# A planned kernel: two-bank copies, short spins, paired score matmuls, a new load plan, and a last store in halves

## The chip, the cores and the metric

The kernel runs on one core of one Trainium2 chip. Times are device microseconds (us) of that core. A kernel is quoted by the median of its fast runs with their range. A ratio is the mean time of one kernel's fast runs over that of the kernel before in the same rounds on the same chip, so it is not quite the ratio of the quoted medians. Executions over 1.5% slower than the fastest of the same kernel are left out of the means. A profile is one execution, and its "span" is some 2 us shorter than the time. TensorE is PE in the profile (PEld: its weight loads), VectorE DVE, ScalarE ACT, GpSimd POOL, SyncE SP.

## The reference

An RWKV5 attention over 24 chunks (4 batch rows, 6 chunks of 128 steps) is followed by a mixture of four experts, each applied to every row.

```python
cur   = einsum('bhd,bhe->bhde', u * k_t, v_t)
y_t   = einsum('bhd,bhde->bhe', r_t, state + cur)
state = w * state + einsum('bhd,bhe->bhde', k_t, v_t)
...
p = domain_probs / (domain_probs.sum(-1) + 1e-9)      # 3072 rows, 4 experts
out += p[:, e] * (relu(x @ w1[e]) @ w2[e])            # 384 -> 1024 -> 384
```

The inputs r, k, v are 4 x 8 x 768 x 48 in fp32. The weights are 12.6 MB in fp32, cast to bf16 on the chip.

## The kernel before

The program is a set of jobs. While it builds, it plays them through on a model of the five engines and the DMA queue, with an assumed duration for each. The order in which jobs begin in that play is the order in which each engine gets its instructions. On the chip the order is fixed, and an engine whose next instruction has no data waits. I call the play "the plan".

```python
def load_in(n, ci):  load_job((n, ci), (0.97, 64), run, ...)              # 192 KB: 0.97 us of queue assumed
def load_w(m, e, i):                                                      # a weight piece of 2 or 3 blocks
    us = 0.615 * (bb - a) + (0.4 if i == 0 else 0.0) + (0.5 if (m, e, i) == (1, 0, 0) else 0.0)
ORDER = "K0 V0 K1 V1 R0 K2 R1 R2 w1e0.0 w1e0.1 K3 ...".split()            # order of the loads on SyncE
...
def cast(m, e, i, rank):      # staged fp32 -> bf16 weights: a job of ACT, DVE or POOL
    job(("cast", m, e, i), on, run, [("wst", m, e, i)], rank, (), (("wst", m, e, i),))
...
# scores of one chunk: both halves of its transposed R and K from one PSUM bank, copied out by ACT and DVE
for q in range(NP):
    for j in range(2):
        nc.tensor.matmul(tl["At", ci, j][:, q, :], ..., start=True, stop=True)   # 8 matmuls, 64 rows
...
spin(NSPIN)                   # 11 filler matmuls of 512 columns at the start, for the clock
for t, _, e, j in started:    # the plan, played out
    if e == "T":
        slow = 2.0 if t < WARM else 1.0
        n = int((t - pe_end - 0.2) / (0.22 * slow) * 0.6)
        if t < 30 and n > 0:
            spin(min(n, 8))   # fillers of 512 columns where the plan has TensorE idle
```

## Time and profile before

| | before |
|---|---|
| time, median of 3 runs | 301.76 us (301.3 to 302.39) |
| span of the profiled run | 299.2 us |
| first scores / first hT / end of last matmul | 10.28 / 18.61 / 295.80 us |
| first expert's second matmul ("out") | 25.84 us |
| end of last matmul to end of span | 3.39 us |

hT is the first matmul of an expert (x times w1), out the second. Y is the attention output of a chunk, X its transpose, from which the experts start. This is the chain of work that ended last, by line, in shares of the span:

```profile
PE out_ps L577 42%; PE hT_ps L550 35%; PE hT_ps L544 5%; PE At_ps L417 3%; PE Y_ps L448 2%; PE RKT_ps L381 1%; DMA Rt<-in_r_dram 1%; DVE w_sb L74 1%; PE Y_ps L441 1%; PE St_ps L489 1%; PE spin_ps L170 1%; SPq L188 1%; DVE RK L324 1%; PE xT_ps L474 1%; DVE S L502 0%
```

The table of windows: length, then busy us and count of PE, PEld, DVE, ACT, POOL; then clock, DMA share, GB/s.

```profile
26.00:60.00 34.00, 33.73 (x347) 22.01 (x348) 29.61 (x53) 22.29 (x36) 16.61 (x21) 1.00 1.01 274
60.00:90.00 30.00, 29.84 (x333) 20.37 (x333) 22.92 (x42) 22.13 (x37) 23.44 (x31) 1.00 0.90 215
```

And the waits between 26 and 92 us (total, times, longest): this is the largest on a load.

```profile
POOL dv L363 <- DMA Vt<-in_v_dram: 10.7, 2, 8.3
```

TensorE is busy for all but 0.4 us of these 64 us, while the DMA queues are about full. There are waits of POOL on inputs.

### The profile page before, as it was taken

To read this page: it belongs to the slowest core of one execution; us is meant where nothing else is said; L and a number is where in the kernel's file an instruction comes from. 1 tells how busy PE (TensorE), PEld (TensorE's weight loads), DVE (VectorE), ACT (ScalarE), POOL (GpSimd) and SP (SyncE) were. 2 spreads that over 40 slices of the span, in tenths; PEclk is the share of its full clock that TensorE was granted. 3 is DMA by queue.
4 is the path that set the end of the run, shared out by engine and by line. 5 is a ranking of instruction groups with operands and counts; after the bars stand their busy time and mean duration, and the time that the engine had idled before them with its cause. 6 is when DMAs were issued, how large, how long until landed. Compare 5 with 4: busy or idle time off the path is not lost.

```text
span 299.2 us, 5668 instructions
## 1 busy us (share of the span) xinstructions
PE 288.9 (97%) x2216; PEld 167.0 (56%) x2244; DVE 157.3 (53%) x299; ACT 152.3 (51%) x253; POOL 100.5 (34%) x136
## 2 busy tenths in 40 slices
PE   7699999999999999999999999999999999999995
PEld 2377557688545655555555455555555555555553
DVE  3776879987866736445556435555414422101223
ACT  5376865585683043554533464434465344565430
POOL 1866164677976623253253244231000000000000
PEclk9789999999999999999999999999999999999999
DMA  7998999998987083662462771421232000200002
GB/s 151 275 306 240 325 246 269 229 241 209 244 174 146 16 186 101 167 127 45 84 127 54 180 129 37 96 49 37 96 71 50 0 13 28 79 0 2 0 0 105
DMA packets 108110, 36.92 MB, mean 123 GB/s; under 512 B 96282, under 2 KB 108060, under 8 KB 108084
## 3 DMA queue, kind: packets, MB, share of 16 engines
q1 hardware_dynamic: 108068, 36.56, 51.1%
q8 instruction: 17, 0.28, 0.4%
q14 instruction: 9, 0.07, 0.1%
q10 hardware_dynamic: 16, 0.00, 0.0%
HBM read 26.79 MB, written 4.72 MB: 105 GB/s over the span
## 4 chain that ended last, share of the span: by engine, by line
PE 91%; DVE 4%; DMA 1%; issue 1%; SPq 1%; ACT 0%; DVEq 0%; ACTq 0%
PE out_ps L577 42%; PE hT_ps L550 35%; PE hT_ps L544 5%; PE At_ps L417 3%; PE Y_ps L448 2%; PE RKT_ps L381 1%; DMA Rt<-in_r_dram 1%; DVE w_sb L74 1%; PE Y_ps L441 1%; PE St_ps L489 1%; PE spin_ps L170 1%; SPq L188 1%; DVE RK L324 1%; PE xT_ps L474 1%; DVE S L502 0%
## 5 line engine op out<-in xcount | busy, mean ns | idle before, releaser
L561 ACT ACTIVATE hTs<-hT_ps 128x512 bf16<-128x512 f32 x168 | 99.6, 598 | 104.5 <-PE hT_ps L550 100.0
L577 PE MATMUL out_ps<-w_sb,hTs 128*128 128x384 bf16 x768 | 140.1, 326 | 0.2 <-DVE w_sb L74 0.2
L550 PE MATMUL hT_ps<-xTe,w_sb 128*128 128x512 bf16 x476 | 122.5, 379 | 1.5
L577 PEld LDWEIGHTS <-hTs 128*128 128x128 bf16 x768 | 72.7, 98 | 52.2 <-DVE w_sb L74 0.7
L587 DVE SCALAR_TENSOR_TENSOR oacc<-out_ps,p_nat,oacc 128x384 f32<-128x384 f32 x72 | 44.3, 617 | 91.3 <-PE out_ps L577 90.2
L550 PEld LDWEIGHTS <-w_sb 128*128 128x128 bf16 x504 | 47.0, 98 | 47.0 <-DVE w_sb L74 0.3
L426 DVE TENSOR_TENSOR AtM<-At_ps,mask 128x512 bf16<-128x512 f32 x48 | 31.0, 684 | 19.8 <-PE At_ps L417 19.8
L363 POOL TENSOR_TENSOR dv<-Vt,dcoef 128x384 f32<-128x384 f32 x24 | 21.5, 896 | 50.8 <-DVE Ysb L457 32.3
L337 POOL TENSOR_TENSOR ruk<-Rt,Kt 128x384 f32<-128x384 f32 x24 | 24.6, 1025 | 40.2 <-DMA Kt<-in_k_dram 33.2
L345 POOL TENSOR_TENSOR ruk<-ruk,U_sd 128x384 f32<-128x384 f32 x23 | 24.0, 1046 | 1.2
L585 ACT ACTIVATE oacc<-out_ps,p_nat 128x384 f32<-128x384 f32 x24 | 14.0, 582 | 14.1 <-PE out_ps L577 13.8
L457 DVE TENSOR_TENSOR Ysb<-Y_ps,dv 128x384 bf16<-128x384 f32 x24 | 13.3, 555 | 13.2 <-PE Y_ps L448 11.3
L559 ACT ACTIVATE hTs<-hT_ps 128x512 bf16<-128x512 f32 x24 | 14.1, 600 | 9.3 <-PE hT_ps L544 8.7
L509 POOL TENSOR_TENSOR S<-Tn,wC 64x192 bf16<-64x192 f32 x32 | 16.1, 503 | 7.1 <-DVE Tn L504 5.9
L544 PE MATMUL hT_ps<-xTe,w_sb 128*128 128x128 bf16 x288 | 18.2, 219 | 0.0
L544 PEld LDWEIGHTS <-w_sb 128*128 128x128 bf16 x288 | 16.6, 98 | 0.9 <-DVE p_nat L294 0.2
L324 DVE TENSOR_TENSOR RK<-Rt,W_sd 128x384 bf16<-128x384 f32 x20 | 14.2, 714 | 0.0
L504 DVE TENSOR_TENSOR Tn<-S,St_ps 64x192 f32<-64x192 bf16 x32 | 11.2, 350 | 5.6 <-PE St_ps L489 4.8
L358 DVE TENSOR_REDUCE dcoef<-ruk 128x8 f32<-128x384 f32 x24 | 13.0, 542 | 0.1
L76 POOL CAST Vb<-Vt 128x384 bf16<-128x384 f32 x20 | 10.7, 541 | 6.5 <-PE St_ps L489 4.9
L72 ACT CAST w_sb<-wst 128x1152 bf16<-128x1152 f32 (+1 forms) x13 | 12.8, 1003 | 0.0
L324 DVE TENSOR_TENSOR RK<-Kt,W_sd 128x384 bf16<-128x384 f32 x20 | 12.7, 635 | 0.0
(63 smaller groups left out, 136.8 us busy)
## 6 DMA issues: line engine op xcount, KB each, us to landing
wst<-in_moe_w_dram SPq DMA_DIRECT2D x16, 576.0 KB, 6.5
Kt<-in_k_dram SPq DMA_DIRECT2D x24, 192.0 KB, 3.9
Vt<-in_v_dram SPq DMA_DIRECT2D x24, 192.0 KB, 5.6
Rt<-in_r_dram SPq DMA_DIRECT2D x24, 192.0 KB, 4.1
out_dram<-oacc SPq DMA_DIRECT2D x24, 192.0 KB, 1.9
wst<-in_moe_w_dram SPq DMA_DIRECT2D x8, 384.0 KB, 5.4
RKT<-RK SPq DMA_TRANSPOSE x14, 3.2
xTe<-Ysb SPq DMA_TRANSPOSE x14, 2.5
```

Source lines behind the costliest of these rows:

```text
L324: eng.tensor_mul(RK[:, i, :, 0:D], tl[("Kt", "Rt")[1 - i], ci], tl["W", i] if ci < SUB and i not in on_pool else W_sd[i])
L337: nc.gpsimd.tensor_mul(tl["ruk", ci], tl["Rt", ci], tl["Kt", ci])
L345: nc.gpsimd.tensor_mul(tl["ruk", ci], tl["ruk", ci], U_sd)
L363: nc.gpsimd.tensor_mul(tl["dv", ci], tl["Vt", ci], tl["dcoef", ci].to_broadcast((128, H, D)))
L426: nc.vector.tensor_mul(tl["AtM", ci][:, j], tl["At", ci, j], mask[:, None, :].to_broadcast((128, NP, C)))
L509: nc.gpsimd.tensor_mul(S_new[pr, :, cl], tl["Tn", ci][pr], wC[pr, :, None].to_broadcast((P2, NP, D)))
L544: nc.tensor.matmul(ps[:, i, :], w1_sb[:, e, db, (fb + i) * 128:(fb + i + 1) * 128], xTe[:, db, s0, :], start=(i == 0 and db == 0), stop=(i ...
L550: nc.tensor.matmul(ps[:, 0:n, :].rearrange("p a b -> p (a b)"), w1_sb[:, e, db, fb * 128:(fb + 1) * 128], xTe[:, db, s0:s0 + n, :].rearran ...
L559: nc.scalar.activation(hTs[:, fb:fb + 4, s0, :], ps, AF.Relu)
L561: nc.scalar.activation(hTs[:, fb, s0:s0 + n, :], ps[:, 0:n, :], AF.Relu)
L577: nc.tensor.matmul(ps, tl["hTs", e, sc][:, fb, s, :], w2_sb[:, e, fb, :], start=(fb == 0), stop=(fb == NFB - 1))
L587: nc.vector.scalar_tensor_tensor(tl["oacc", ci], in0=tl["o", e, ci], scalar=pe, in1=tl["oacc", ci], op0=ALU.mult, op1=ALU.add)
```

## The change

The intent: let the two copies of a transpose result overlap (two PSUM banks in place of one), fill TensorE's idle time at the start with shorter spins so that the clock stays up, pay the entry and exit of a score stretch once for two chunks, shorten the last evacuation and store, and take a new load order. With the load order come shorter assumed load durations, 5% less for inputs and 14% less for weights.

```diff
-        load_job((n, ci), (0.97, 64), run, (("inp", ci),))
+        load_job((n, ci), (0.92, 64), run, (("inp", ci),))
...
-        us = 0.615 * (bb - a) + (0.4 if i == 0 else 0.0) + (0.5 if (m, e, i) == (1, 0, 0) else 0.0)
+        us = 0.53 * (bb - a) + (0.3 if i == 0 else 0.0) + (0.5 if (m, e, i) == (1, 0, 0) else 0.0)
...
-    ORDER = ("K0 V0 K1 V1 R0 K2 R1 R2 w1e0.0 w1e0.1 K3 w1e0.2 V2 R3 w2e0.0 w2e0.1 p V3 w2e0.2 R4 K4 "
+    ORDER = ("R1 R0 K1 V1 K0 V0 K2 w1e0.0 R2 w1e0.1 w1e0.2 R3 V2 p K3 w2e0.0 V3 w2e0.1 R4 K4 w2e0.2 "
...                                                            (the rest of the order differs too)
+            two = ci < SUB
...
+                    if two:
+                        tl["T", ci, i] = psum.tile([128, NP, C], BF16, tag=("tr", "At")[i], bufs=i + 1,
+                                                   name="RKT_ps")
...
+        paired = ci >= DMAT
...
+            for x in (ci - 1, ci) if paired else (ci,):
+                for j in range(2):
+                    tag = ("tr", "mm")[j] if paired and x == ci else "At"
...
+            if (e, ci) == (E - 1, TOTC - 1):
+                last_chunk(e, ci, rk + 2, groups)     # second matmul, evacuation, store: two halves
+                continue
...
-                slow = 2.0 if t < WARM else 1.0
-                n = int((t - pe_end - 0.2) / (0.22 * slow) * 0.6)
-                if t < 30 and n > 0:
-                    spin(min(n, 8))
+                n = int((t - pe_end - 0.05) / 0.056)
+                if t < 24 and n > 0:
+                    spin(n, 1)                        # one block of 128 columns, not four
```

Not shown: RKT gets four buffers for three, Tn two for three, and the first chunk of a pair moves to the slot of the second.

## The prediction

> **What bounds the kernel now.** I read the page first: busy shares, the row of the granted clock, and the chain that ended last.
>
> ```profile
> PE 288.9 (97%) x2216; PEld 167.0 (56%) x2244; DVE 157.3 (53%) x299; ACT 152.3 (51%) x253; POOL 100.5 (34%) x136
> ...
> PEclk9789999999999999999999999999999999999999
> ...
> PE 91%; DVE 4%; DMA 1%; issue 1%; SPq 1%; ACT 0%; DVEq 0%; ACTq 0%
> ```
>
> TensorE (PE) is 97% busy and 91% of the chain that sets the end; no other engine passes 53%. The clock row has one dip, in its second and third slice. So the kernel is matmul bound, and only what shortens TensorE's sequence, or starts it earlier, can count. The table of windows tells where TensorE is not doing real work:
>
> ```profile
> 5.00:10.00 5.00, 2.70 (x14) 1.08 (x13) 1.78 (x4) 2.44 (x6) 1.41 (x2) 1.00 1.07 199
> 10.00:15.00 5.00, 3.93 (x40) 2.52 (x41) 4.04 (x9) 2.09 (x6) 4.83 (x6) 0.55 1.01 316
> 15.00:20.00 5.00, 5.00 (x55) 3.42 (x54) 3.58 (x8) 3.52 (x6) 3.15 (x4) 0.76 1.12 301
> ...
> 100.00:150.00 50.00, 49.68 (x343) 27.21 (x347) 26.49 (x50) 22.61 (x38) 17.89 (x25) 1.00 0.49 107
> ```
>
> From 100 us on TensorE lacks 0.3 us in 50. But in 5:10 it is busy for 2.70 us of 5, in 10:15 for 3.93 at a granted clock of 0.55, in 15:20 all the time but at 0.76. Finer windows (a quarter of a microsecond each) put the dip from 10.5 to 17.35 us, at 0.50 throughout. I added up what the sequence needs at the full-clock spacings of the trace (out 768 x 0.1625 us, 512-wide hT 504 x 0.216, 128-wide hT 288 x 0.056, At 24 visits x 0.42, Y 24 x 0.20 + 20 x 0.17, state 20 x 0.17, transposes 110 x 0.056, set-up 2.3): 280.0 us. The last matmul issues at 295.6, so 15.6 us are lost, 6.8 of them before the first transpose at 8.28 us, some 7 between there and the first expert matmul at 18.61, and only about 2 in all the rest. The start shows why, in the timeline of all engines:
>
> ```profile
> 9.17 0.59 ACT L72 COPY RKT<-RKT_ps 128x512 bf16<-128x512 bf16 x1 [1.80 <-PE RKT_ps L381]
> ...
> 9.79 0.42 DVE L74 COPY RKT<-RKT_ps 128x512 bf16<-128x512 bf16 x1 [0.50 <-ACT RKT L72]
> ...
> 14.87 1.03 PE L381 MATMUL RKT_ps<-ident,RK 128*128 128x128 bf16 x8
> ...
> 15.70 2.28 PE L170 MATMUL spin_ps<-spin_in 128*128 128x512 bf16 x6
> 15.94 0.42 DVE L74 COPY RKT<-RKT_ps 128x512 bf16<-128x512 bf16 x1 [1.35 <-PE RKT_ps L381]
> ...
> 16.40 0.59 ACT L72 COPY RKT<-RKT_ps 128x512 bf16<-128x512 bf16 x1 [0.75 <-DVE RKT L74]
> ...
> 16.74 1.28 DVE L426 TENSOR_TENSOR AtM<-At_ps,mask 128x512 bf16<-128x512 f32 x2
> 16.88 1.89 ACT L72 CAST w_sb<-wst 128x1152 bf16<-128x1152 f32 x2
> ...
> 18.61 0.84 PE L544 MATMUL hT_ps<-xTe,w_sb 128*128 128x128 bf16 x12
> ```
>
> The two copies of one transpose result never overlap: at 9.79 VectorE (DVE) had waited for ScalarE (ACT), at 16.40 ScalarE for VectorE, 0.5 and 0.75 us. The eight transposes at 14.87 take 1.03 us at half clock. Six filler matmuls ("spins") take 2.28 us. The cast of the second weight piece, which the first hT needs, starts only at 16.88, behind the delayed copy. Further on the cost of a score visit can be read from TensorE's timeline:
>
> ```profile
> 155.50 0.81 PE L550 MATMUL hT_ps<-xTe,w_sb 128*128 128x512 bf16 x3
> 156.25 0.40 PE L417 MATMUL At_ps<-RKT 64*128 64x128 bf16 x8
> 156.57 0.82 PE L550 MATMUL hT_ps<-xTe,w_sb 128*128 128x512 bf16 x3
> ```
>
> Three hT issue from 155.50 and are done issuing after 3 x 0.216 at 156.15; the scores start at 156.25 and the next hT at 156.57. The visit costs 0.42 us. Its eight matmuls start within 0.40 - 0.216 = 0.18 us, so eight are worth 0.21, and 0.21 is the price of going in and out. Last, the end:
>
> ```profile
> 295.83 0.62 DVE L587 SCALAR_TENSOR_TENSOR oacc<-out_ps,p_nat,oacc 128x384 f32<-128x384 f32 x1 [0.68 <-PE out_ps L577]
> ```
>
> After this evacuation of 0.62 us the last store is issued at 296.48; its packets run from 297.31 to 297.99, the landing is seen at 298.33, and the span ends at 299.2.
>
> **What the Trainium skill says.** TensorE: Matmul & The Clock Gate, Part 1 (the HAM clock gate): the clock is either full or half, set by how busy TensorE was in a free-running window, about 3.4 us long. The trace agrees on the two levels (0.50 and 1.00, nothing between); its one low stretch lasts 6.83 us, twice that window. TensorEngine Tiling (Array Packing), Key Properties: changing the tiling mode drains TensorE. The trace agrees: 64-row scores between 128-row matmuls pay the 0.21 us. PSUM — Partial Sum Buffer, section PSUM bank collisions raise a hardware error: two engines must not touch one bank at once, even to read, so the program orders them by bank. The trace agrees: the 0.5 and 0.75 us waits between the copies. DMA: Bandwidth & Descriptors, Anatomy of one DMA: a fixed part of about 2 us, mostly the write receipt, that halving a transfer leaves alone. Here 1.85 us pass from issue to landing, 0.68 of them packets.
>
> **The change, part by part.**
>
> *Scores in pairs.* The instruction order of the changed kernel has ten score stretches of 8 and seven of 16, no other matmul within a stretch. A pair should cost 0.21 + 2 x 0.21 = 0.63 in place of 0.84, so 7 x 0.21 = **1.5 us** off a saturated TensorE. The cost is one of the four "mm" banks until the fourth mask is done, 4 x 0.68 + 0.2 = 3 us later. In the order, three hT (1.95 us) and an out (1.3) follow the pair, then Y and more; the waits listed for them are on ScalarE's relus and on an evacuation that precedes the masks in VectorE's order. Y of the second chunk comes about 5.9 us after the pair. I expect no stall, at most 0.1 us a pair.
>
> *The last chunk in halves.* TensorE does the same columns (16 x 0.0825 for 8 x 0.1625). The last evacuation has half the elements: about 0.42 for 0.62 if some 0.2 us of it are fixed, an estimate. The last store's packets take half: -0.3. **0.45 us**.
>
> *The start.* Loads begin R1 R0 K1 V1 K0 V0; K0, which completes chunk 0, is the fifth load as R0 was before, so lands at the same 7.57. R of chunk 0 is scaled and transposed before it. From there I walk the new orders of each engine with the durations of the trace, the clock taken as full; a load is taken to land when the trace had moved as many bytes as stand ahead of its end in the new order, plus the 0.8 us that R of chunk 0 took from its last byte (6.78) to its use (7.57). K scaled to 8.22, its transposes done at 8.7; VectorE does ruk (to 9.3), then its copy (9.7); ScalarE has V0's cast first (V0 lands sixth, about 8.7), then its copy, to 9.87. Scores at 9.93 (10.28 before). Masks behind two reductions 10.8 to 12.1; Y at 12.2 (12.45). Copies of chunk 1 in parallel by 13.75, X of chunk 0 at 13.9 behind 17 spins, scores of chunk 1 at 14.2. Their masks now precede the next copy on VectorE: 14.8 to 16.1 (before 16.74 to 18.02). ScalarE casts piece one at 11.75 and piece two, landing about 14.2, by 15.4. So the first hT runs at about **15.9**, 2.7 us earlier. Then masks, POOL's scale of K3 (its load lands at 18) and two copies of chunk 3 on ScalarE pace it: the sixth hT group, after which all first hT of three chunks, four transposes and four score visits are done, ends near 23.5; the same work is done at 25.84 in the kernel before (its four small p transposes included). Gain **2.3 us**. After that the second-matrix pieces, then expert 1's, are needed 2.3 us earlier, while the DMA queues are nearly full (share 1.0 from 10 to 24, one hole at 24 to 26). I let 0.5 us go there: **1.8 us**.
>
> Sum with a full clock: 301.8 - 1.5 - 0.45 - 1.8 = 298.0.
>
> **The rivals.**
>
> *The clock still drops.* 100 spins of 128 columns take 5.6 us at full clock, but 30 of them stand between the first scores and Y, 17 before X. At half clock these are 3.2 and 1.8 us: Y moves from 12.2 to 13.5, X to 16.6, the first hT to about 19, so the start loses some 0.5 us instead of gaining. For it: spins cannot fill the wait for K0 (7.4 to 8.3), and before, a window that was 56% busy was not enough. Against it: the same stretch becomes about 77% busy, by the walk above. Result 300.3. I give it 0.3.
>
> *The start's gain is hidden by weights.* If expert 0's second matrix and expert 1's pieces arrive no earlier, TensorE waits in 24 to 36 us for what it gained, and only 1.5 + 0.45 and perhaps 0.5 remain: 299.3. For it: the DMA share. Against it: the hole at 24 to 26, and only 0.8 us of TensorE loss in 25 to 45 before.
>
> *The shared bank stalls TensorE.* If each pair costs the 0.2 us that it saves, the pairs are worth nothing and the time is 299.5. The order's waits speak against it, and four score banks masked in one go hold VectorE for 2.7 us only where it was 53% busy.
>
> **Range and chances.** The full-clock case (0.7) centres on 298.0, the half-clock case on 300.3, either with the weights as a spread of about 1 us. I predict **298.3 us**, 8 times in 10 from **296.5** to **300.6**. Two per cent faster is 295.7; for that the start would have to yield over 4 us of the 9 lost there after 8.28, which the casts forbid: 0.06. Slower by 2% would need a stall at every pair and a lost start: 0.02. Within 2%: 0.92.
>
> **What would show it.** Right: seven score stretches where the gap from the last hT issued to the next is 0.63; no TensorE idle time over 0.1 us after them; a granted clock of 1.00 from about 4 us on; the first hT near 15.9; copies of one chunk that overlap; a last evacuation near 0.42 and a last store with 0.34 us of packets. Wrong: a clock row with a 6.8 us dip, spins on the chain of waits before Y or X, waits of out_ps or hT_ps on casts between 23 and 36 us, or waits of hT_ps on masks.

## The result, and the profile after

The changed kernel takes **302.12 us** (301.87 to 302.36, 4 runs), the kernel before 301.88 us in the same rounds; the ratio is 1.0008 (95% interval 0.9988 to 1.0029). It is the same within 2%, as I gave 0.92 to, but the time lies outside the range of 296.5 to 300.6. The profiled span is 300.1 us against 299.2.

The page of the changed kernel, busy shares, clock row and the two lines of the chain:

```profile
PE 294.4 (98%) x2342; PEld 174.1 (58%) x2342; DVE 154.3 (51%) x299; ACT 153.5 (51%) x253; POOL 102.5 (34%) x137
...
PEclk9999999999999999999999999999999999999999
...
PE 92%; DVE 4%; DMA 2%; SPq 1%; issue 0%; ACT 0%; DVEq 0%
PE out_ps L624 39%; PE hT_ps L594 36%; PE spin_ps L170 4%; PE hT_ps L588 4%; PE At_ps L428 2%; DMA wst<-in_moe_w_dram 2%; PE RKT_ps L386 2%; DVE RK L324 1%; PE Y_ps L466 1%; PE St_ps L507 1%; PE Y_ps L459 1%; SPq L200 1%; PE u_ps L257 1%; PE w_ps L253 1%; PE out_ps L557 0%
```

TensorE looks even busier, and the clock row has no dip. Two things stand out in the chain: spins, 4% where they were 1%, and weight loads (wst), 2%, which the chain before did not have. The clock row misleads: its first record in this run comes at 13.86 us. How long TensorE's work took says what the clock was before, in the timeline:

```profile
9.44 1.35 PE L170 MATMUL spin_ps<-spin_in 128*128 128x128 bf16 x11
...
13.83 1.85 PE L170 MATMUL spin_ps<-spin_in 128*128 128x128 bf16 x30
...
16.14 0.42 DVE L74 COPY RKT<-RKT_ps 128x512 bf16<-128x512 bf16 x1 [0.46 <-PE RKT_ps L386]
...
16.36 0.59 ACT L72 COPY RKT<-RKT_ps 128x512 bf16<-128x512 bf16 x1 [2.53 <-PE RKT_ps L386]
...
19.03 0.83 PE L588 MATMUL hT_ps<-xTe,w_sb 128*128 128x128 bf16 x12
```

Eleven spins take 1.35 us at 9.44, 0.12 each; thirty take 1.85 us at 13.83, 0.06 each. So the clock was half until 13.86, where the kernel before had it released at 3.70 and then lost it from 10.5 to 17.35. The copies at 16.14 and 16.36 do overlap, as intended. The first hT comes at 19.03, not 18.61.

The windows of the changed kernel, start, weight time and steady state:

```profile
5.00:10.00 5.00, 5.00 (x16) 1.82 (x15) 1.03 (x2) 1.99 (x5) 1.99 (x2) 1.00 1.03 209
10.00:15.00 5.00, 5.00 (x61) 4.61 (x59) 2.97 (x6) 3.00 (x7) 3.03 (x4) 1.00 1.12 334
15.00:20.00 5.00, 5.00 (x99) 4.63 (x95) 4.40 (x10) 3.12 (x6) 3.47 (x4) 1.00 1.06 251
26.00:60.00 34.00, 33.70 (x384) 23.85 (x382) 28.29 (x55) 24.54 (x37) 17.83 (x25) 1.00 1.04 278
60.00:90.00 30.00, 28.74 (x300) 18.95 (x299) 22.95 (x39) 18.13 (x28) 22.36 (x26) 1.00 0.90 216
100.00:150.00 50.00, 50.00 (x356) 27.58 (x354) 24.51 (x49) 23.79 (x40) 20.05 (x28) 1.00 0.53 111
```

From 60 to 90 us TensorE is busy 28.74 us where it was 29.84. The waits between 26 and 92 us have two lines at their top that the kernel before has not:

```profile
DVE w_sb L74 <- DMA wst<-in_moe_w_dram: 6.9, 4, 2.6
ACT w_sb L72 <- DMA wst<-in_moe_w_dram: 6.0, 4, 2.8
```

A cast that waits doesn't stop TensorE by itself, but what stands behind it in the same engine's order does. The timelines of DVE, ACT and TensorE at 81 to 87 us:

```profile
81.33 1.14 DVE L74 CAST w_sb<-wst 128x768 bf16<-128x768 f32 x1 [2.62 <-DMA wst<-in_moe_w_dram]
...
84.08 0.83 ACT L72 CAST w_sb<-wst 128x768 bf16<-128x768 f32 x1 [2.85 <-DMA wst<-in_moe_w_dram]
...
84.94 0.68 DVE L437 TENSOR_TENSOR AtM<-At_ps,mask 128x512 bf16<-128x512 f32 x1
...
86.07 0.68 DVE L437 TENSOR_TENSOR AtM<-At_ps,mask 128x512 bf16<-128x512 f32 x1
...
86.80 0.27 PE L466 MATMUL Y_ps<-Vb,AtM 128*128 128x48 bf16 x4 [0.85 <-DVE AtM L437]
```

DVE stood still for 2.62 us until the weights of that cast were there; the masks of scores that were done at 80.9 came after it and after two more jobs, and Y waited 0.85 us for the second mask.

The score stretches of two chunks, in TensorE's timeline:

```profile
158.86 1.46 PE L624 MATMUL out_ps<-w_sb,hTs 128*128 128x384 bf16 x8
160.26 0.62 PE L428 MATMUL At_ps<-RKT 64*128 64x128 bf16 x16
160.81 2.12 PE L594 MATMUL hT_ps<-xTe,w_sb 128*128 128x512 bf16 x9
```

Eight out issue until 158.86 + 8 x 0.1625 = 160.16, and hT starts at 160.81: 0.65 us for two chunks, for which the kernel before paid 2 x 0.42. And the last evacuation is 0.42 us where it was 0.62:

```profile
297.07 0.42 DVE L562 SCALAR_TENSOR_TENSOR oacc<-out_ps,p_nat,oacc 128x192 f32<-128x192 f32 x1 [0.24 <-PE out_ps L557]
```

To see where the time went I kept the ledger of the prediction running: each matmul counts as its full-clock spacing, in the order in which it issues (records missing from a trace filled in from the program's order), and "lost" is the time passed minus that. Spins count nothing. Unlike in the prediction's 280.0 us, eight score matmuls count as 0.21 us here, so that the way in and out of a score stretch is in "lost".

| lost by TensorE, us | to 26 us | 26 to 90 us | 90 to 290 us | last matmul to span's end |
|---|---|---|---|---|
| before | 15.84 | 1.96 | 2.96 | 3.39 |
| changed | 16.62 | 3.80 | 1.53 | 3.07 |
| difference | +0.78 | +1.84 | -1.43 | -0.32 |

The sum, +0.87, is the difference of the two spans (+0.91) but for the few us after 290 that are left out. The late gains came almost as predicted; the start gained nothing in this run, and 1.84 us went between 26 and 90 us.

### The profile page after: what moved, and what is told of

Its sections match the earlier page's. It is cut to its first block, busy times and chain, and to the rows that moved or that the text cites. A ratio compares the mean times of both kernels' runs of the same rounds, so it can differ in the third digit from the quotient of the medians.

```text
span 300.1 us, 5903 instructions
## 1 busy us (share of the span) xinstructions
PE 294.4 (98%) x2342; PEld 174.1 (58%) x2342; DVE 154.3 (51%) x299; ACT 153.5 (51%) x253; POOL 102.5 (34%) x137
## 2 busy tenths in 40 slices
DMA packets 108255, 36.94 MB, mean 123 GB/s; under 512 B 96298, under 2 KB 108204, under 8 KB 108228
## 4 chain that ended last, share of the span: by engine, by line
PE 92%; DVE 4%; DMA 2%; SPq 1%; issue 0%; ACT 0%; DVEq 0%
PE out_ps L624 39%; PE hT_ps L594 36%; PE spin_ps L170 4%; PE hT_ps L588 4%; PE At_ps L428 2%; DMA wst<-in_moe_w_dram 2%; PE RKT_ps L386 2%; DVE RK L324 1%; PE Y_ps L466 1%; PE St_ps L507 1%; PE Y_ps L459 1%; SPq L200 1%; PE u_ps L257 1%; PE w_ps L253 1%; PE out_ps L557 0%
## 5 line engine op out<-in xcount | busy, mean ns | idle before, releaser
L437 DVE TENSOR_TENSOR AtM<-At_ps,mask 128x512 bf16<-128x512 f32 x48 | 30.3, 682 | 25.0 <-PE At_ps L428 25.0
L363 POOL TENSOR_TENSOR dv<-Vt,dcoef 128x384 f32<-128x384 f32 x24 | 20.2, 843 | 43.8 <-DVE Ysb L475 30.7
L632 ACT ACTIVATE oacc<-out_ps,p_nat 128x384 f32<-128x384 f32 x24 | 13.9, 582 | 15.6 <-PE out_ps L624 15.6
L527 POOL TENSOR_TENSOR S<-Tn,wC 64x192 bf16<-64x192 f32 x32 | 18.1, 564 | 7.1 <-DVE Tn L522 5.9
L72 ACT CAST w_sb<-wst 128x1152 bf16<-128x1152 f32 (+1 forms) x13 | 13.7, 1051 | 6.1 <-DMA wst<-in_moe_w_dram 6.0
L170 PE MATMUL spin_ps<-spin_in 128*128 128x128 bf16 (+1 forms) x111 | 13.9, 285 | 1.1 <-DVE spin_in L90 1.1
L324 DVE TENSOR_TENSOR RK<-Kt,W_sd 128x384 bf16<-128x384 f32 x20 | 13.9, 695 | 0.1
L324 DVE TENSOR_TENSOR RK<-Rt,W_sd 128x384 bf16<-128x384 f32 x20 | 13.7, 685 | 0.2
```

The lines of the kernel that those rows point to most:

```text
L170: nc.tensor.matmul(ps[:, 0:m, :], spin_in, spin_in[:, None, :].to_broadcast((128, m, 128)), start=True, stop=True)
L324: eng.tensor_mul(RK[:, i, :, 0:D], tl[("Kt", "Rt")[1 - i], ci], tl["W", i] if ci < SUB and i not in on_pool else W_sd[i])
L363: nc.gpsimd.tensor_mul(tl["dv", ci], tl["Vt", ci], tl["dcoef", ci].to_broadcast((128, H, D)))
L437: nc.vector.tensor_mul(tl["AtM", ci][:, j], tl["At", ci, j], mask[:, None, :].to_broadcast((128, NP, C)))
L527: nc.gpsimd.tensor_mul(S_new[pr, :, cl], tl["Tn", ci][pr], wC[pr, :, None].to_broadcast((P2, NP, D)))
```

## The experiments

**Theory A:** the start's gain is lost because the clock was released at 13.86 us instead of some 4 us; release it in time, and the predicted time comes. **Theory B:** what the start gains is given back between 26 and 90 us, because weights do not arrive earlier and the fixed orders of DVE and ACT make TensorE wait behind casts. Later experiments split B: is it the new load order, or the shorter assumed durations? The three sets of runs were on three chips; before took 301.39, 301.69 and 301.35 us there (7 runs each).

### 1. A longer opening: after_spin15

```diff
-    WARM, NSPIN = 5.4, 11
+    WARM, NSPIN = 5.4, 15
```

> The changed kernel with 15 opening spins in place of 11, nothing else. In the profile of the changed kernel the clock was released at 13.86 us, in that of before at 3.70, and the 11 spins ended at 5.7 at half clock. Fifteen spins at 0.427 us keep TensorE on 128-row matmuls beyond 7.04, the end of the next window. Theory A, the late release is what ate the start: clock 1.00 from about 7.0, first scores near 10.9 in place of 13.3, first hT 16.3 to 16.6 in place of 19.0, and the time 1.5 to 2.5 us below the changed kernel's 302.1, so 299.6 to 300.6. Rival B, the waits on weights at 70 to 90 us set the end whatever the start does: first hT as early, but the loss at 70 to 90 grows from 2.3 us and the time stays within 0.5 of 302.1. Rival C, more spins only delay: first hT later, time up by 1 us.

Measured: 302.63 us (301.89 to 303.57), ratio 1.0042 (1.0005 to 1.008). In its profile the clock is released at 4.17 us and stays. Scores start at 9.93, Y at 11.94, X at 13.55, the first hT at 15.47. The walk of the prediction had 9.93, 12.2, 13.9 and 15.9, so it was right for a full clock. The ledger to 26 us stands 1.67 us better than before. And yet the last matmul ends at 297.06, as in the changed kernel (297.03): 6.30 us are lost between 26 and 90. The waits of casts are now the largest:

```profile
ACT w_sb L72 <- DMA wst<-in_moe_w_dram: 12.8, 8, 4.1
DVE w_sb L74 <- DMA wst<-in_moe_w_dram: 10.5, 6, 2.9
```

TensorE's window from 60 to 90 us is no better than the 28.74 us of the changed kernel:

```profile
60.00:90.00 30.00, 28.25 (x293) 18.77 (x296) 22.90 (x39) 18.00 (x28) 22.43 (x27) 1.00 0.96 228
```

What TensorE gained, the casts waited longer. Theory A falls as the cause of the miss; B stands, with the size still to be shown.

### 2. The old spin rule: after_oldspins

The changed kernel with the spin rule of the kernel before (the last lines of the diff undone).

> The changed kernel with the old spins (512 columns, few) in place of the short ones, the rest as changed. The new loads give back what the start wins or loses (theory B), so the time stays within 0.7 of 302.1, though the clock shows a half-rate dip again (mean clock under 0.99) and the first hT moves to anywhere from 16 to 19.5. Rival: short spins carry the start, and without them the time rises by over 1 us.

Measured: 302.24 us (300.4 to 303.05), ratio 1.0012 (0.9969 to 1.0055). The clock dips from 8.22 to 11.64, but the first hT is at 15.18 and the last matmul ends at 297.11; casts wait 21.6 us for weights. So short spins are not what makes the early start (the rest of the change is enough), and the gain is given back just the same. No run undoes the two-bank copies alone.

### 3. No pairs: after_nopairs

```diff
-        paired = ci >= DMAT
+        paired = False
...
-            e_g, sc_g, one = SLOTS[ci - LEAD - (ci % 2 if ci >= DMAT else 0)]
+            e_g, sc_g, one = SLOTS[ci - LEAD]
```

> The changed kernel with the pairing of the scores undone (every score stretch of 8 matmuls, two banks), nothing else. If a pair saves the price of one way in and out, 7 x 0.21, the time rises by 1.5 us to 303.6, and TensorE's loss at 100 to 250 us rises from 1.3 to 2.7. If the shared bank cost as much as it saved, the time stays at 302.1.

Measured: 303.59 us (301.97 to 304.24), ratio 1.0065 (1.0022 to 1.0107), 1.5 us over the changed kernel's 302.12. The ledger from 100 to 250 us is 2.90 us lost against 1.31: 1.6 us for seven pairs, 0.23 each. The two times are from two chips and the intervals of their ratios overlap; it is the ledger that shows the gain.

### 4. The late parts alone: before_pairs_halves

The kernel before with the pairs and the last chunk in halves, and nothing else of the change.

> The kernel before with the paired scores and the halved last chunk alone; spins, copies and loads as before. If the parts add: 301.9 - 1.5 (pairs) - 0.3 (halves, as measured in the two profiles: 3.07 from the last matmul's end to the end of the span, 3.39 before) = 300.1. If the pairing only works with the new loads or disturbs the old schedule: 301.9 or above.

Measured: 300.05 us (298.51 to 300.34), ratio 0.9945 (0.9905 to 0.9985), though its clock dips from 9.02 to 19.26. 0.55% of 301.4 is 1.7 us; the ledger gave 1.43 + 0.32. The late parts do what they should. The whole change, which has them too, is at 1.0008, so everything else in it costs time on the whole.

### 5. The whole last chunk: wholelast

```diff
-            if (e, ci) == (E - 1, TOTC - 1):
+            if False:
```

> The changed kernel with the last chunk's second matmul, evacuation and store whole, as before. From the end of the last matmul to the end of the span: 3.07 us in halves in the changed kernel, 3.39 whole in the kernel before. If the halves are the reason, 3.3 to 3.5 here; if the end differs by chance from run to run, 3.0 to 3.2. The time itself can't resolve 0.3 us in one look.

One look: 301.75 us. From the last matmul's end to the span's end it takes 3.38 us, against 3.07 in halves: 0.31 us is the halves' worth. The last evacuation there is

```profile
296.61 0.62 DVE L634 SCALAR_TENSOR_TENSOR oacc<-out_ps,p_nat,oacc 128x384 f32<-128x384 f32 x1 [0.68 <-PE out_ps L624]
```

so 0.20 of it is the evacuation. The remaining 0.1 is what the packets can have saved: whole, the last store's 192 KB run alone from 298.08 to 298.76; in halves, its packets run in one stretch with those of the store before it, from 297.22 to 298.79.

This run shows one more thing by chance. With the same opening as the changed kernel, its clock was released at 5.70 us. Its first hT is at 15.36, its ledger to 26 us is 13.84, 2.0 us better than before; and then it loses 6.10 us to 90. The sum is the same time. Whether its clock is released early or late, the changed kernel stands 2.1 to 2.7 us behind the kernel before at 90 us (15.84 + 1.96 = 17.80 us lost there; 20.42 in its own profile, 19.94 here, 20.47 in experiment 1).

### 6. The old load plan: after_oldloads, and with 15 opening spins: oldloads_spin15

The changed kernel with the load order and the assumed durations of the kernel before; the second also has NSPIN = 15.

```diff
-        load_job((n, ci), (0.92, 64), run, (("inp", ci),))
+        load_job((n, ci), (0.97, 64), run, (("inp", ci),))
-        us = 0.53 * (bb - a) + (0.3 if i == 0 ...
+        us = 0.615 * (bb - a) + (0.4 if i == 0 ...
-    ORDER = ("R1 R0 K1 V1 K0 V0 K2 w1e0.0 R2 ...
+    ORDER = ("K0 V0 K1 V1 R0 K2 R1 R2 w1e0.0 ...
```

> The changed kernel with the order of the loads and the assumed load durations of the kernel before, the rest as changed. Theory B, the new order places casts on VectorE and ScalarE ahead of data that lands late (VectorE sat 2.6 us in front of a cast at 81, Y waited 0.9 behind it): TensorE's loss at 70 to 90 us falls from 2.3 to about 0.7 and the time by 1 to 1.6 us, to 300.5 to 301.1, even with a late clock. Theory A alone: the loss at 70 to 90 stays about 2 and the time within 0.5 of 302.1. The start cannot be better than with the new order by more than 0.5.

Measured: 300.62 us, in two groups (299.66 and 299.81; 301.42 and 301.48), ratio 0.9964 (0.9917 to 1.0011). The profiled run is of the slow group, with the clock released at 13.69. That the two groups are early and late releases is likely, but only this one profile shows it. No cast waits for weights.

> The changed kernel with the old load order and load durations and 15 opening spins. With the new loads, an early clock (4.17 us) won 2.45 us by 26 us and had lost all of it by 90, where casts waited 23 us for weights; with the old loads no cast waited in 26 to 90 and the runs fell in two groups, 299.7 and 301.4, the profiled slow one with the clock released only at 13.7. Theory B (with the old loads the start is not given back): all runs in the fast group, 299.2 to 300.0, and TensorE's loss at 26 to 90 below 2.5 us. Rival (supply of weights is the limit in either order): no faster than 301, loss at 26 to 90 above 3.5.

Measured: **299.55 us** (298.86 to 300.54), ratio 0.9934 (0.99 to 0.9967): faster than both kernels, by less than 1%, and the fastest correct version together with experiment 4, whose interval overlaps. Two of the four runs lie outside the 299.2 to 300.0 that I expected, and the loss between 26 and 90 us is 2.76, not below 2.5; the rival (301, above 3.5) is still out. The clock is released at 3.76. No cast waits for weights between 26 and 92 us. TensorE's window:

```profile
60.00:90.00 30.00, 29.84 (x324) 20.21 (x326) 21.49 (x42) 20.57 (x33) 24.34 (x33) 1.00 0.97 228
```

But this version does not keep a gain of the start, for it hardly has one. Its first hT comes at 17.12 us, its ledger to 26 us is only about 0.3 us better than before, and it then loses 0.8 more to 90, with one wait of 1.30 us for a cast of expert 0's second matrix that stands behind a late V in POOL's order:

```profile
26.71 0.65 PE L624 MATMUL out_ps<-w_sb,hTs 128*128 128x384 bf16 x3 [1.30 <-POOL w_sb L76]
```

Its whole gain over the kernel before comes from the pairs and the halves. So the early start comes only with the new load plan, and no correct version both has it and keeps it.

### 7. Order or durations: after_oldorder_newtimes and after_slowertimes

The first is the changed kernel with the old order and the new durations. The second has the new order with durations close to the old ones: 0.97, 0.58 per block and 0.4 for 0.92, 0.53 and 0.3. (The new order with exactly the old durations doesn't build: the plan runs into a deadlock.)

> The changed kernel with the old load order but the new, shorter assumed durations of the loads. If the durations are what puts casts too early: casts wait for weights in 26 to 90 us (over 6 us in sum; 12.9 in the changed kernel, none with old order and old durations), loss at 26 to 90 above 3 us, time 301.5 to 302.5. If the order is the cause: waits of casts under 3 us, loss about 2, time as with old loads, 299.7 to 301.4.

Measured: 304.07 us (the three fast runs, 301.97 to 304.25; one slow run of 306.67), ratio 1.006 (1.0011 to 1.0109). The profiled run is slow, so only its waits are read: casts wait 7.1 us for weights, where the same order with the old durations had none.

> The changed kernel with its new load order but longer assumed durations (0.97 us an input load, 0.58 a third of a weight piece plus 0.4; the old values exactly do not schedule). The counterpart: if the durations are the cause, the casts' waits on weights at 26 to 90 fall from 12.9 to below 5 us and the time to 300 to 301.3; if the order is the cause, the waits stay above 8 us and the time at 302.

Measured: 310.01 us (308.41 to 311.76), ratio 1.028 (1.023 to 1.0329), the only version that is slower by more than 2%. Casts wait 14.9 us for weights. TensorE's worst window, with the clock at half from 74.9 to 88.6 us:

```profile
60.00:90.00 30.00, 23.11 (x224) 16.44 (x225) 15.38 (x29) 15.15 (x23) 21.12 (x27) 0.77 0.78 200
```

Both times came out above what I expected. The shorter durations do harm in the old order too: casts wait, as expected if the durations are to blame, and the ratio is 1.006 against 0.9964 for after_oldloads (intervals that just touch). Against the whole change (1.0008) the first version is not clearly worse. The second says that longer durations do not save the new order. I then printed the plan itself while the kernels were built and set it beside the traces. Last casts are read from the traces directly; the landing of the loads is counted from the queue's packets of each kind, good to about 1 us, and the lateness is that of the loads planned before 95 us.

| | planned end of last matmul | measured | last cast of DVE / ACT: planned | measured | largest lateness of a load |
|---|---|---|---|---|---|
| before | 294.85 | 295.80 | 79.1 / 87.7 | 81.1 / 89.8 (no wait for weights) | 1.8 us |
| changed | 292.07 | 297.03 | 74.3 / 77.2 | 81.3 / 84.1 (waited 2.6 / 2.9) | 8.7 us |
| oldloads_spin15 | 294.34 | 294.87 | | | 0.5 us |
| old order, new durations | 293.27 | (slow) | | | 10.6 us |
| new order, slower durations | 303.62 | 306.93 | | | 2.8 us |

This fits the four whose ends can be compared. With the old durations the loads come between 3.8 us sooner and 1.8 us later than planned. With the new ones the plan of the changed kernel lets the last weight load and V13 (the V of chunk 13, the last load of the listed order) end at 76.7 and 77.6 us; the trace has them at 83.6 and 84.3. The plan of the changed kernel ends 2.8 us earlier than the one before, but on weights that don't come. Given slower durations, the new order makes a plan that is bad on its own terms (303.62).

### 8. A third of the weights: spin15_third, with a control

Experiment 1's kernel, in which the weight loads of experts 1 to 3 bring a third of a piece (half, for a two-block piece of the second matrix), and the cast reads that part two or three times. The result is wrong; the order of instructions is unchanged.

```diff
+            if e and m == 1:
+                nc.sync.dma_start(t[:, 0:(bb - a) * 128], w1_v[e][:, 0, a * 128:bb * 128])
+            elif e:
+                nc.sync.dma_start(t[:, 0:Dm], w2_v[e][:, a, :])
...
+            if e and m == 1:
+                copy_on(eng, w1_sb[:, e, :, a * 128:bb * 128],
+                        t[:, None, 0:n * 128].to_broadcast((128, NDB, n * 128)))
+            elif e:
+                copy_on(eng, w2_sb[:, e, a:bb, :], t[:, None, 0:Dm].to_broadcast((128, n, Dm)))
```

> The changed kernel with 15 opening spins, and every weight load of experts 1 to 3 cut to a third of its bytes (the casts read that third three times or twice; the result is wrong on purpose; order of instructions and casts unchanged; expert 0's loads, so the start, unchanged). Theory B, the start's gain is given back because weights arrive too late for the casts: the casts' waits for weights between 26 and 92 us go from 23 us to under 3, TensorE's loss between 26 and 90 us from 6.3 to about 2.5, last matmul end near 293.5, time about 299 (298 to 300), against 302.6. Rival, it is the order of jobs itself (casts, masks, state) that stalls TensorE, whatever arrives: waits for weights fall but the loss stays over 5 us and the time within 1 us of 302.6.

Measured: **296.51 us** (296.34 to 296.89), ratio 0.9845 (0.9822 to 0.9868), 6.1 us under experiment 1. The loss between 26 and 90 us falls from 6.30 to 2.60. Of the 23 us of cast waits one wait is left:

```profile
ACT w_sb L72 <- DMA wst<-in_moe_w_dram: 3.0, 1, 3.0
```

and TensorE's window is full, at a lower DMA share:

```profile
60.00:90.00 30.00, 30.00 (x317) 19.77 (x316) 25.71 (x44) 18.46 (x30) 24.53 (x30) 1.00 0.63 128
```

The last casts start at 74.9 and 77.5 us (planned 74.3 and 77.2), and the last matmul ends at 292.06 us, where the plan has 292.07. That close is luck, but it says what the change lacks: the loads. The gain exceeds what I expected (299), partly because the loss before 26 us also fell, from 14.17 to 13.03; expert 1's pieces are on the queue by then.

> Control: the same cut of the weight loads in the kernel with 15 opening spins, the earlier load order and the earlier assumed durations, whose casts waited for no weight. Theory B: nothing to win by earlier weights, within 0.7 us of 299.55, loss between 26 and 90 us 2 to 3 us. Rival, smaller loads help in another way (less traffic for input chunks and stores): over 1.5 us faster than 299.55.

Measured: 299.36 us (298.73 to 299.81), ratio 0.994 (0.9916 to 0.9964), against 0.9934 with full loads. In a plan that does not count on early weights, cutting them gains nothing, so lighter traffic is not by itself what helped in spin15_third. Theory B is shown for the loads as a whole. The inputs stand on the same queue as the weights, so the cut brings them earlier too: POOL's waits on inputs between 26 and 92 us fall from 17.6 us in experiment 1 to 5.7. The kernel before had 13.8 us of such waits and lost only 1.96, so they need not cost much; but the share of each is not separated, nor is the part of the lateness that SyncE's own waits for other engines add (in the changed kernel 3.5, 3.4 and 2.6 us are the largest between 5 and 90 us).

## Why the prediction was wrong, by its own steps

**The bound.** Right: TensorE is 91% and 92% of the chain that sets the end in the two kernels, and the ledger of its losses accounts for their difference to 0.04 us.

**Pairs, 1.5 us.** Right: 1.43 in the ledger of 90 to 290 us, 1.5 in time when undone. No pair stalls; the rival of the shared bank is out.

**Halves, 0.45 us.** 0.31 measured. The evacuation was right (0.42); the -0.3 for the packets was about -0.1, as far as one look tells: the halves' packets run in one stretch with the store before.

**The start with a full clock.** The walk was right where the clock was full: first hT at 15.36 and 15.47 in two profiles, predicted 15.9. Its worth at 26 us was 2.0 and 1.7 us for the 2.3 of the text.

**"The clock taken as full", 0.7.** It failed in the profiled run of the changed kernel, by a late release and not by the dip I had named. There the first hT came at 19.03 and the start lost 0.78 us: the half-clock case of the text, about 19 and some 0.5, so that these two numbers agree by luck. But it isn't what decided the time, since with the clock released in time (after_spin15, wholelast) the time is the same.

**"I let 0.5 us go there".** This is the step that failed. The text names the mechanism as a rival, that weights arriving no earlier hide the start's gain, and prices it at 0.5 us in the sum and at most the start's whole gain as a rival (299.3). It looked at 24 to 36 us, where the trace before had a hole in the DMA queue. In the runs the loads land up to 8.7 us later than the plan has them, and the loss from 26 to 90 us rises by 4.3 and 4.1 us in the two profiles with a clock released in time (experiments 1 and 5), by 1.84 in that with a late one. From 26 to 36 us, where I had looked, it is 0.9 and 0.6 of that; the rest follows up to 90. It is not bounded by the start's gain either: the fixed orders put masks, evacuations and copies behind casts on DVE and ACT, so that a cast that comes 7 us after its planned time holds up work that was ready. In place of -1.8 the start and what follows from it gave +2.1 to +2.7 in the ledgers. That difference, 3.9 to 4.5 us, is the whole miss of 3.8 us (302.12 against 298.3), to within what single profiles differ.

**What I could have read before the run.** The plan of the kernel before had its last weight load and V13 land at 87.2 and 88.2 us, and its trace had them at 89.0 and 88.7 (loads in the middle of the plan came up to 3.8 us sooner). At the end there was nothing to shorten. A change that assumes 14% less for each weight piece on a queue already at a share of 1.01 had to be checked against that. The diff showed the numbers, and I did not print the plan.

## What to carry to other kernels

Where a program plans its order from assumed durations, compare the planned with the measured start of each job; with one assumed too short, engines that work in a fixed order put work that is ready behind work that isn't. (A longer one is not safe of itself: the new order with longer durations took 310.01 us.) A gain at the start of a kernel is kept only if every later supplier (here the loads of the next 60 us) can come as much earlier, so price it at each later wait and not at the first one. Test it by making the supply cheaper on purpose, with a control that does not depend on it.

## What the Trainium skill lacked or had wrong

- TensorE: Matmul & The Clock Gate, Part 1, says that the clock is released after at least one busy window of about 3.4 us and that the moment varies with the window's phase by 0.5 us. Here the same eleven opening spins, started at 1.05 us, released it at 3.70 in the profile of the kernel before, but at 13.86 in that of the changed kernel and at 5.70 in that of the same kernel with a whole last chunk: 10.2 us of variation, three windows. The page does not say how full a window has to be. Counted back from the release in steps of 3.41 us (the dips of the clock in these profiles last 3.4, 6.8, 10.2 or 13.7 us), in the twelve profiles that have a clock record, the window that released it had 2.64 us or more of matmuls, and no window before it more than 2.57, if the four setup matmuls with a single row in fp32 are left out: 2.64 in the kernel before, but 2.57, 2.31 and 1.51 and only then 3.41 in the changed one. That is an inference from these profiles, not an experiment. In the late case matmuls stood in TensorE's record without a gap from 5 to 10 us, among them the four in fp32, which took 3.28 us; that such matmuls count little as activity would explain it, but no run here isolates it.
- The clock row of the profile is full from its first slice in the changed kernel, while eleven spins of 128 columns took 0.12 us each at 9.44 us and 0.06 each at 13.83. The same page warns of unreliable clock records; there is simply no record before the first release, and none at all in the profile of after_nopairs.
- DMA: Bandwidth & Descriptors, Bandwidth, gives 341 GB/s for 1 MB transfers issued by GpSimd. This kernel's queue, issued by SyncE and full of inputs in 192-byte rows and weight pieces (96,298 of its 108,255 packets are under 512 bytes), moved 274 to 278 GB/s from 26 to 60 us at a share of 1.01 to 1.04. The page says that small descriptors are slow, but has no figure for such a mix, and with the shorter durations loads landed up to 8.7 us after the plan.
- The same page, Anatomy of one DMA, has a fixed part of about 2 us and one that goes with the size, for DMAs issued by GpSimd. The last store before, issued by SyncE, took 1.85 us from issue to landing, 0.68 of it packets, so 1.17 for the rest. Halving it gained some 0.1 us, not half of the 0.68; its packets ran in one stretch with those of the store before it.
- TensorEngine Tiling (Array Packing), Key Properties, says that a change of mode drains TensorE, without a price: here 0.42 us for a stretch of eight 64-row matmuls and 0.65 us for sixteen, so about 0.2 us for each visit.
- No page tells of an order planned with assumed durations, and what an optimistic one costs: 3.1 us between experiment 1 (302.63) and the same kernel with the old load plan (299.55), and 6.1 to the same order with two thirds of the later weight bytes cut (296.51, result wrong).
